# The last 64 contraction rows of a gated feed-forward as two half-array tiles

## Chip, cores and metric

The kernel runs on one core of a Trainium2 chip. The metric is device time in microseconds (us); before, three runs gave a median of 827.28 us (827.27 to 827.48).

## What is computed

The input x has 2048 rows of 448 columns, float32. Each row is normalised to xn. From xn come a Fourier mixing s and a gated feed-forward g, and the output is x + s * g.

```python
xn = layernorm(x)
a, b = xn @ hid_re.T, xn @ hid_im.T
s = seq_re @ a - seq_im @ b
g = silu((gelu(xn @ w_gate) * (xn @ w_up)) @ w_down)
out = x + s * g
```

The gate and up weights are 448 x 1792, the down weight 1792 x 448; the sequence matrices are 2048 x 2048. This case is about the two products `xn @ w_gate` and `xn @ w_up`, whose contraction has 448 rows: three tiles of 128 and a rest of 64.

## The kernel before

**Split operands.** Every float32 operand is split into two float32r parts, a high part h and a low part l. ScalarE (ACT) copies the operand into h with rounding, VectorE (DVE) subtracts to get l. A product is h\*h + h\*l + l\*h, summed in one PSUM bank. For a contraction of 448 rows that makes 3 x 3 = 9 full passes for the first 384 rows. The last 64 rows are stored twice, in partitions 0 to 63 and again in 64 to 127 of the fourth tile, on both sides. For the weights the first copy holds h and the second l (`prep_w`, L137), so that two full passes, one against xn's high part and one against its low part, do h\*h, l\*h, h\*l and l\*l of these rows. One tile of gate or up therefore takes 11 passes (`gu_mm`, L154 to L164).

**Tiling.** The 2048 rows form four chunks c of 512; xn is held transposed in SBUF for all of them, as xth[c] and xtl[c]. The hidden width 1792 is 14 tiles f of 128, worked off in seven groups of two (`GROUPS`). For each tile and chunk there are two PSUM banks, pg[0] for gate and pg[1] for up. They come from a pool of four banks (`ps_mm`). `act` (L170) then applies gelu to the gate on ACT, multiplies by up on DVE, and splits the result into h and l of hs (L172, L175, L176, L177).

**Down.** `down` (L190) multiplies hs by the down weights: four row tiles kk, six passes of 448 columns each, and DVE adds the sum of each into gacc (L210; in group 0 it copies, L208). The banks are two of `ps_o` and two of `ps_tp`; in group 0 only the two of `ps_o`. Functions in the list `between` are called behind the row tiles, which places other engines' work among down's.

**Order.** Every engine runs its instructions in the order in which they are written. After a start that is written out by hand (L215 to L342), a loop runs over the groups gi and chunks c (L346 to L385). One round before is: gate and up of the group's first tile, `down` of the previous round (`prev`), preparation of something for the next group (the weights of its two tiles in rounds 1 and 2, its down weights in round 3; in the last group the hidden-DFT matrices eh and el), then gate and up of the second tile with its `act`. SyncE (SP) issues all DMAs; the load for a preparation is issued at the head of its round into one of three raw buffers.

**The start.** L338 prepares the first weight of group 1. Its copy runs on ACT, its two subtractions on GpSimd (POOL). Behind it stand the Newton step of the layernorm (L89 to L93) and the norms of chunk 3 (L101), three on DVE and one on POOL.

**After the loop** come the hidden products (`hid_mm`, L401) with 22 passes per row tile, which read eh[0] to eh[3] in turn. The first of them is issued ahead of the last `down`. Then come the sequence products (L466 to L468).

Of the kernel before, what the change touches and what calls it, by code (L numbers as in the profile page):

```python
# [13 lines left out]
P = 128  # L14
S = 2048
D = 448
DX = 512             # D and its last 64 columns again
F = 1792
NK = S // P          # 16 row tiles; row r = p * 16 + k
NC = 4               # chunks of four row tiles  # L20
NF = F // P          # 14 tiles of the hidden width
EPS = 1e-5
WARM = 10
GROUPS = [(f, f + 1) for f in range(0, NF, 2)]
# [1 line left out]

@with_exitstack
def fnet_geglu(ctx: ExitStack, tc: tile.TileContext, x, ct, et, wgu, wd, out):
    """xn = layernorm(x); s = Cr (xn ErT) - Ci (xn EiT);
    g = silu((gelu(xn Wg) * (xn Wu)) Wd); out = x + s * g.  # L30

    float32 operands of products are split into two float32r parts, h + l, exactly; a product is
    h*h + h*l + l*h in one PSUM accumulation. A contraction of 448 rows is three tiles of 128 and
    one of 64, whose h*h and l*h (and h*l and l*l) share a tile.

    Every engine runs its instructions in the order in which they stand here."""
    nc = tc.nc

    xv = x.rearrange("p (k d) -> p k d", k=NK)
# [11 lines left out]
    def big(shape, dt, name):  # L51
        return bigp.tile(shape, dt, name=name, tag="big")
# [7 lines left out]
    def split(h, l, src):  # L60
        nc.scalar.activation(h, src, AF.Copy)  # L61
        nc.vector.tensor_sub(l, src, h)  # L62

# [1 line left out]
    xr, xth, xtl = [None] * NC, [None] * NC, [None] * NC  # L65

    def load_x(c, k0, k1):
# [4 lines left out]
    def stats(c, k0, n):  # L72
        st = const.tile([P, 4, 6], F32, name=f"st{c}_{k0}", tag="st", bufs=2)
        mv = const.tile([P, 4, 2], F32, name=f"mv{c}_{k0}", tag="mv", bufs=3)
        sd = const.tile([P, 4, 4], F32, name=f"sd{c}_{k0}", tag="sd", bufs=3)

        def one(i):
            nc.vector.bn_stats(st[:, i], xr[c][:, k0 + i, :D])  # L78
            nc.vector.bn_aggr(mv[:, i], st[:, i])

        def root():
            r, t, w = sd[:, :n, 0], sd[:, :n, 1], sd[:, :n, 2]
            nc.scalar.activation(t, mv[:, :n, 1], AF.Sqrt, bias=epst)
            nc.vector.tensor_scalar(w, mv[:, :n, 1], EPS, -0.5, op0=ALU.add, op1=ALU.mult)  # L84
            nc.vector.tensor_scalar_mul(sd[:, :n, 3], mv[:, :n, 0], -1.0)

        def newton():
            r, t, w = sd[:, :n, 0], sd[:, :n, 1], sd[:, :n, 2]
            nc.vector.reciprocal(r, t)  # L89
            # one Newton step: r * (1.5 - 0.5 * (var + eps) * r * r)  # L90
            nc.vector.tensor_mul(t, r, r)  # L91
            nc.vector.tensor_mul(t, t, w)
            nc.vector.scalar_tensor_tensor(r, t, 1.5, r, op0=ALU.add, op1=ALU.mult)  # L93

        def norm(i, eng=nc.vector):
            v = xr[c][:, k0 + i]
            if eng is nc.scalar:
                eng.activation(v, v, AF.Identity, bias=sd[:, i, 3:4])
                eng.activation(v, v, AF.Copy, scale=sd[:, i, 0:1])
            else:  # L100
                eng.tensor_scalar(  # L101
                    v, v, mv[:, i, 0:1], sd[:, i, 0:1], op0=ALU.subtract, op1=ALU.mult
                )

        return one, root, newton, norm
# [12 lines left out]
        xth[c] = big([P, 4, 512], FR, f"xth{c}")  # L118
        xtl[c] = big([P, 4, 512], FR, f"xtl{c}")

# [1 line left out]
    def load_w(f):  # L122
        raw = raw_tile(f"wraw{f}")
        nc.sync.dma_start(raw, wgu[f].rearrange("p k g f -> p (k g f)"))
# [2 lines left out]
    def prep_w(f, raw, copy=None, sub=None):  # L127
        w = big([P, 1792], FR, f"w{f}")
        wh, wl = w[:, :1024], w[:, 1024:]
        if copy is None:  # L130
            nc.scalar.activation(wh, raw, AF.Copy)
        else:
            copy(wh, raw)
        sub = sub or nc.vector.tensor_sub
        sub(wl, raw[:, :768], wh[:, :768])
        # the last 64 contraction rows: h below, l above
        sub(wh[64:, 768:], raw[64:, 768:], wh[64:, 768:])  # L137
        return wh, wl

    def load_d(grp):  # L140
# [7 lines left out]
    def prep_d(grp, rv, sub=None):  # L148
        w = big([P, 2, 2, D], FR, f"d{grp[0]}")
        nc.scalar.activation(w[:, 0], rv, AF.Copy)  # L150
        (sub or nc.vector.tensor_sub)(w[:, 1], rv, w[:, 0])
        return w

    def gu_mm(ps, w, g, c, cols, late_xtl=False):  # L154
        wh, wl = w
        hs = [wh[:, (2 * k + g) * P : (2 * k + g + 1) * P] for k in range(4)]
        ls = [wl[:, (2 * k + g) * P : (2 * k + g + 1) * P] for k in range(3)]
        hh = [(hs[k], xth[c], k) for k in range(3)]
        hl = [(hs[k], xtl[c], k) for k in range(3)]
        lh = [(ls[k], xth[c], k) for k in range(3)]  # L160
        last = [(hs[3], xth[c], 3), (hs[3], xtl[c], 3)]
        mm = hh + lh + last[:1] + hl + last[1:] if late_xtl else hh + hl + lh + last
        for n, (a, xt, k) in enumerate(mm):
            nc.tensor.matmul(ps[:, cols], a, xt[:, k, cols], start=n == 0, stop=n == len(mm) - 1)  # L164

    def gu_ps(f, c):
        pool, tag = (ps_o, "po") if (f, c) == (0, 1) else (ps_mm, "mm")
# [12 lines left out]
    def gateup(f, c, w, hs, between=()):  # L180
        pg = gu_ps(f, c)
        for g in range(2):
            gu_mm(pg[g], w, g, c, slice(0, 512))
            if g < len(between):
                between[g]()
        return act(f, c, pg, hs)
# [24 lines left out]
            if kk < len(between):  # L211
                between[kk]()

# [1 line left out]
    with tc.manual_schedule():  # L215
        load_x(0, 0, 1)
        load_x(0, 1, 2)
# [14 lines left out]
        tbl = const.tile([P, 1], F32, name="tbl")  # L232
        nc.scalar.activation(tbl, epst, AF.Sqrt)

        # keep the tensor engine's clock up while the first rows come in
        warm = ps_o.tile([P, 512], F32, name="warm", tag="po")
        for _ in range(WARM):
            nc.tensor.matmul(warm, junk[:, :P], junk, start=True, stop=True)
# [96 lines left out]
        one(3)  # L335
        l1()
        root()
        nws = [prep_w(GROUPS[1][0], w_raw[0], None, nc.gpsimd.tensor_sub)]  # L338
        newton()
        for i in range(4):  # L340
            norm(i, nc.gpsimd if i == 3 else nc.vector)
        prev = (0, 1, wdn, hs1)  # L342

# [1 line left out]
        eh, el = [], []  # L345
        for gi, grp in enumerate(GROUPS):  # L346
            nxt = GROUPS[gi + 1] if gi + 1 < len(GROUPS) else None
            if gi > 0:
                nws = []
            for c in range(NC) if gi > 0 else range(2, NC):  # L350
                if nxt and c in (1, 2):
                    raw = load_w(nxt[c - 1])
                elif nxt and c == 3:
                    raw = load_d(nxt)
                elif not nxt:
                    raw = raw_tile(f"eraw{c}")[:, : 2 * D]
                    nc.sync.dma_start(raw, et[c].rearrange("p r d -> p (r d)"))
                hs = big([P, 2, 2, 512], FR, f"hs{gi}_{c}")
                m0, h0, l0 = gateup(grp[0], c, ws[0], hs[:, 0])
                between, between1 = [lambda: (m0(), h0()), l0], []  # L360
                if (gi, c) == (0, 2):
                    new_xt(3)
                    turn = lambda k: turn_split(*turn_mm(3, k))
                    between = [between[0], lambda: (l0(), turn(0)), lambda: turn(1), lambda: turn(2)]
                    between1 = [lambda: turn(3)]
                down(*prev, between)
                if nxt and c in (1, 2):
                    nws.append(prep_w(nxt[c - 1], raw))
                elif nxt and c == 3:
                    nwdn = prep_d(nxt, raw)  # L370
                elif not nxt and c < 3:
                    eh.append(ring_tile(f"eh{c}", 0))
                    el.append(ring_tile(f"el{c}", 1))
                    split(eh[c][:, : 2 * D], el[c][:, : 2 * D], raw)
                elif not nxt:
                    eh.append(raw_tile("eh3", FR))
                    nc.scalar.activation(eh[3][:, : 2 * D], raw, AF.Copy)
                    nc.vector.tensor_sub(eh[3][64:, : 2 * D], raw[64:], eh[3][64:, : 2 * D])
                m1, h1, l1 = gateup(grp[1], c, ws[1], hs[:, 1], between1)
                m1()  # L380
                h1()
                l1()
                prev = (gi, c, wdn, hs)
            if nxt:
                ws, wdn = nws, nwdn  # L385

# [1 line left out]
        ab = [None] * NK  # L388

        def hid_mm(k):  # L390
# [20 lines left out]
                l[:, 1], ps[1], -1.0, h[:, 1], op0=ALU.mult, op1=ALU.subtract  # L411
            )

        # pieces of Cr, Ci: four row tiles of s by one of t
        pieces = [(tt, q) for tt in range(NK) for q in range(4)]
        c_raw, c_hl = {}, {}

# [30 lines left out]
        hid_split(NK - 1, ps)  # L448
        load_c(2)

# [1 line left out]
        for n, (tt, q) in enumerate(pieces):  # L452
            load_c(n + 3)
            split_c(n + 2)
# [60 lines left out]
```

## Time and profile before

| | |
|---|---|
| median of three runs | 827.28 us |
| the profiled execution, first to last instruction (span) | 825.4 us |
| TensorE passes (PE) and weight loads (PEld) | 3932 each |
| mean granted TensorE clock | 0.996 of full |
| one chunk of a later group | 14.87 us |

The profiled execution's own time is known only as this span; what the runs have beyond it, 1.9 us of the median, lies around the first and last instruction.

Times of rows are in us from the span's start. In a timeline row the first number is the start and the second the length of a run of like instructions, xN their count, and the bracket the idle time before them with what ended it. In a row of grouped instructions the last figures are busy time in us, mean ns of one, and idle time before them. L164 is line 164 of the kernel. PE is TensorE's matmul, PEld its weight load, which overlaps it. The ends of matmuls are modelled by the profiler.

### The profile page before, as it was taken

How to read it: one execution, taken by the hardware profiler on the slowest of the kernel's cores; microseconds unless marked ns; L12 is line 12 of the kernel's file. 1: busy time of each engine (PE TensorE's matmuls, PEld its weight loads, DVE VectorE, ACT ScalarE, POOL GpSimd, SP SyncE). 2: the span in 40 equal slices, each digit the busy share in tenths (PEclk: the TensorE clock that was granted, in tenths of full speed). 3: DMA queues.
4: the chain of work that ended last, by engine and by line, in shares of the span. 5: the costliest groups of instructions: out<-in, count | busy, mean ns of one | idle time of the engine just before them, and what ended most of it. 6: DMA issues, size and time to landing. Idle time of an engine off the chain costs nothing.

```text
span 825.4 us, 9169 instructions
## 1 busy us (share of the span) xinstructions
PE 815.2 (99%) x3932; PEld 727.9 (88%) x3932; DVE 311.6 (38%) x464; ACT 204.7 (25%) x280; POOL 46.3 (6%) x30
## 2 busy tenths in 40 slices
PE   7999999999999999999999999999999999999998
PEld 6988888888888888888889999999999999999997
DVE  7983433434334343353443233222323322222321
ACT  3552122121212221222221223122222222222220
POOL 3120000000000000000000000011111111111110
PEclk8999999999999999999999999999999999999999
DMA  8011010010000000001010002344444434343442
GB/s 343 8 40 34 1 52 22 5 48 23 25 26 23 26 25 23 23 23 44 1 47 6 0 26 61 92 138 146 144 136 134 135 125 125 125 125 124 125 125 60
DMA packets 19369, 58.07 MB, mean 70 GB/s; under 512 B 2048, under 2 KB 8064, under 8 KB 18944
## 3 DMA queue, kind: packets, MB, share of 16 engines
q1 hardware_dynamic: 19328, 57.48, 22.0%
q8 instruction: 31, 0.51, 0.3%
q14 instruction: 10, 0.08, 0.0%
HBM read 53.81 MB, written 3.67 MB: 70 GB/s over the span
## 4 chain that ended last, share of the span: by engine, by line
PE 96%; DVE 2%; DMA 1%; issue 0%; ACT 0%; SPq 0%
PE gu L164 33%; PE po L201 16%; PE py L467 13%; PE py L466 13%; PE py L468 13%; PE ab L401 9%; DMA xr<-x 1%; DVE xr L101 1%; PE pt L110 1%; DVE xtl L62 0%; DVE st L78 0%; DVE sd L84 0%; DVE ga L208 0%; DVE sd L91 0%; SPq L70 0%
## 5 line engine op out<-in xcount | busy, mean ns | idle before, releaser
L164 PE MATMUL gu<-xth,w 128*128 128x512 f32 (+1 forms) x826 | 218.9, 383 | 1.9 <-ACT xth L61 1.9
L466 PE MATMUL py<-ab,c 128*128 128x448 f32 x512 | 187.0, 365 | 0.0
L468 PE MATMUL py<-ab,c 128*128 128x448 f32 x512 | 187.0, 365 | 0.0
L467 PE MATMUL py<-ab,c 128*128 128x448 f32 x512 | 187.0, 365 | 0.0
L164 PEld LDWEIGHTS gu<-xth,w 128*128 128x128 f32 x826 | 152.4, 191 | 30.3 <-ACT xth L61 2.1
L201 PE MATMUL po<-d,hs 128*128 128x448 f32 x672 | 142.1, 366 | 1.3 <-DVE ga L208 1.3
L164 PE MATMUL gu<-xtl,w 128*128 128x512 f32 (+1 forms) x472 | 140.8, 381 | 0.0
L201 PEld LDWEIGHTS po<-d,hs 128*128 128x128 f32 x672 | 125.8, 188 | 12.6 <-DVE ga L208 1.5
L62 DVE TENSOR_TENSOR c<-raw,c 128x1024 fp32r<-128x1024 f32 x64 | 78.3, 1224 | 138.1 <-ACT c L61 136.2
L61 ACT ACTIVATE c<-raw 128x1024 fp32r<-128x1024 f32 x64 | 67.9, 1061 | 224.3 <-DMA raw<-ct 217.4
L468 PEld LDWEIGHTS py<-ab,c 128*128 128x128 f32 x512 | 96.2, 188 | 7.6
L466 PEld LDWEIGHTS py<-ab,c 128*128 128x128 f32 x512 | 96.2, 188 | 7.6
L467 PEld LDWEIGHTS py<-ab,c 128*128 128x128 f32 x512 | 96.2, 188 | 7.6
L164 PEld LDWEIGHTS gu<-xtl,w 128*128 128x128 f32 x472 | 87.7, 191 | 16.9
L210 DVE TENSOR_TENSOR ga<-ga,po 128x448 f32<-128x448 f32 x96 | 59.5, 620 | 110.2 <-PE po L201 110.2
L176 ACT ACTIVATE hs<-gt 128x512 fp32r<-128x512 f32 x56 | 35.4, 632 | 180.0 <-DVE gt L175 180.0
L175 DVE TENSOR_TENSOR gt<-gt,gu 128x512 f32<-128x512 f32 x56 | 38.3, 684 | 89.7 <-PE gu L164 89.7
L473 POOL TENSOR_TENSOR ga<-ga,xres 128x448 f32<-128x448 f32 x15 | 31.0, 2067 | 719.2 <-DVE ga L472 719.2
L172 ACT ACTIVATE gt<-gu 128x512 f32<-128x512 f32 x56 | 33.4, 599 | 119.6 <-PE gu L164 119.6
L177 DVE TENSOR_TENSOR hs<-gt,hs 128x512 fp32r<-128x512 f32 x56 | 38.8, 694 | 20.2 <-ACT hs L176 18.3
L472 DVE TENSOR_TENSOR ga<-ga,py 128x448 f32<-128x448 f32 (+1 forms) x17 | 10.1, 594 | 86.5 <-PE py L468 86.5
L401 PE MATMUL ab<-eh,xth 128*128 128x448 f32 x128 | 31.1, 365 | 0.0
(56 smaller groups left out, 332.3 us busy)
## 6 DMA issues: line engine op xcount, KB each, us to landing
raw<-ct SPq DMA_DIRECT2D x64, 512.0 KB, 4.9
wraw<-wgu SPq DMA_DIRECT2D x14, 512.0 KB, 3.6
xres<-x SPq DMA_DIRECT2D x16, 224.0 KB, 5.2
out<-ga SPq DMA_DIRECT2D x15, 224.0 KB, 2.0
draw<-wd SPq DMA_DIRECT2D x7, 448.0 KB, 3.5
xr<-x SPq DMA_DIRECT2D x3, 1024.0 KB, 12.3
eraw<-et SPq DMA_DIRECT2D x4, 448.0 KB, 3.4
xr<-x SPq DMA_DIRECT2D x2, 256.0 KB, 2.9
```

The costliest lines, as they stand in the source:

```text
L61: nc.scalar.activation(h, src, AF.Copy)
L62: nc.vector.tensor_sub(l, src, h)
L164: nc.tensor.matmul(ps[:, cols], a, xt[:, k, cols], start=n == 0, stop=n == len(mm) - 1)
L175: lambda: nc.vector.tensor_mul(gt, gt, pg[1]),
L176: lambda: nc.scalar.activation(hs[:, 0], gt, AF.Copy),
L177: lambda: nc.vector.tensor_sub(hs[:, 1], gt, hs[:, 0]),
L201: nc.tensor.matmul(po[:, :D], hs[:, i, part, kk * P : (kk + 1) * P], wdn[:, b, i], start=n == 0, stop=n == 5,)
L210: nc.vector.tensor_add(ga, ga, po[:, :D])
L401: nc.tensor.matmul(p[:, :D], a, b, start=n == 0, stop=n == len(mm) - 1)
L466: nc.tensor.matmul(py[:, :D], a, h, start=k + r == 0, stop=False)
L467: nc.tensor.matmul(py[:, :D], a, l, start=False, stop=False)
L468: nc.tensor.matmul(py[:, :D], b, h, start=False, stop=q == 3 and i == 7)
```

## The change

Groups 1 to 6 get another way of doing gate and up; group 0, and with it the start, keeps the old one.

- A weight is now split in full: `prep_w_halves` makes h and l for all 1024 columns (one ACT copy, one DVE subtraction), in place of h and 768 columns of l with a packed rest. It is used for all weights from group 1 on, so the first of them (L338) has its subtraction moved from POOL to DVE.
- `gu_main` issues the nine full passes of one tile of gate or up. `gu_tails` issues the last 64 rows of one hidden tile: three products, each for gate on partitions 0 to 63 and for up on partitions 64 to 127, six passes of 64 contraction rows in alternation. The term l\*l of these rows is no longer summed.
- A round is now: the full passes of both tiles, the half passes of both tiles, gelu and product of both, `down` of the previous round with the low parts of hs placed among its sums, then the preparation (`prepare`, which holds the old code).

The comments and the docstring go as well.

```diff
+    def prep_w_halves(f, raw):
+        w = big([P, 2048], FR, f"w{f}")
+        wh, wl = w[:, :1024], w[:, 1024:]
+        nc.scalar.activation(wh, raw, AF.Copy)
+        nc.vector.tensor_sub(wl, raw, wh)
         return wh, wl
...
+    def gu_main(ps, w, g, c):
+        wh, wl = w
+        sl = [slice((2 * k + g) * P, (2 * k + g + 1) * P) for k in range(3)]
+        mm = [(wh, xth[c]), (wh, xtl[c]), (wl, xth[c])]
+        for n, (a, xt) in enumerate(mm):
+            for k in range(3):
+                nc.tensor.matmul(ps, a[:, sl[k]], xt[:, k], start=n + k == 0, stop=False)
+
+    def gu_tails(pg, w, c):
+
+        wh, wl = w
+        mm = [(wh, xth[c]), (wh, xtl[c]), (wl, xth[c])]
+        for n, (a, xt) in enumerate(mm):
+            for g in range(2):
+                rows = slice(64 * g, 64 * g + 64)
+                nc.tensor.matmul(
+                    pg[g], a[rows, (6 + g) * P : (7 + g) * P], xt[rows, 3],
+                    start=False, stop=n == 2,
+                )
...
-        nws = [prep_w(GROUPS[1][0], w_raw[0], None, nc.gpsimd.tensor_sub)]
+        nws = [prep_w_halves(GROUPS[1][0], w_raw[0])]
         newton()
...
+        def prepare(nxt, c, raw):
+            if nxt and c in (1, 2):
+                nws.append(prep_w_halves(nxt[c - 1], raw))
+            elif nxt and c == 3:
+                nwdn.append(prep_d(nxt, raw))
...
                 hs = big([P, 2, 2, 512], FR, f"hs{gi}_{c}")
+                if gi > 0:
+                    pgs = [gu_ps(f, c) for f in grp]
+                    for i in range(2):
+                        for g in range(2):
+                            gu_main(pgs[i][g], ws[i], g, c)
+                    for i in range(2):
+                        gu_tails(pgs[i], ws[i], c)
+                    m0, h0, l0 = act(grp[0], c, pgs[0], hs[:, 0])
+                    m1, h1, l1 = act(grp[1], c, pgs[1], hs[:, 1])
+                    m0()
+                    m1()
+                    h0()
+                    h1()
+                    down(*prev, [l0, l1])
+                    prepare(nxt, c, raw)
+                    prev = (gi, c, wdn, hs)
+                    continue
                 m0, h0, l0 = gateup(grp[0], c, ws[0], hs[:, 0])
```

More of the change, by code (lines that the diff above doesn't have):

```diff
@@ L138, in prep_w @@
         return wh, wl
+    def prep_w_halves(f, raw):
[3 more added lines that the diff above has]
+        nc.vector.tensor_sub(wl, raw, wh)
+        return wh, wl
     def load_d(grp):
@@ L345, in fnet_geglu @@
         eh, el = [], []
+        def prepare(nxt, c, raw):
[3 more added lines that the diff above has]
+                nwdn.append(prep_d(nxt, raw))
+            elif not nxt and c < 3:
+                eh.append(ring_tile(f"eh{c}", 0))
+                el.append(ring_tile(f"el{c}", 1))
+                split(eh[c][:, : 2 * D], el[c][:, : 2 * D], raw)
+            elif not nxt:
+                eh.append(raw_tile("eh3", FR))
+                nc.scalar.activation(eh[3][:, : 2 * D], raw, AF.Copy)
+                nc.vector.tensor_sub(eh[3][64:, : 2 * D], raw[64:], eh[3][64:, : 2 * D])
         for gi, grp in enumerate(GROUPS):
@@ L349, in fnet_geglu @@
                 nws = []
+            nwdn = []
             for c in range(NC) if gi > 0 else range(2, NC):
@@ L366, in fnet_geglu @@
                 down(*prev, between)
[L367 to L378, printed above, removed]
+                prepare(nxt, c, raw)
                 m1, h1, l1 = gateup(grp[1], c, ws[1], hs[:, 1], between1)
@@ L384, in fnet_geglu @@
             if nxt:
-                ws, wdn = nws, nwdn
+                ws, wdn = nws, nwdn[0]
         ab = [None] * NK
```

## The prediction

> **What bounds the kernel now.** I read the page's part 1 first, then its part 4, then the chain in order of time.
>
> ```profile
> span 825.4 us, 9169 instructions
> PE 815.2 (99%) x3932; PEld 727.9 (88%) x3932; DVE 311.6 (38%) x464; ACT 204.7 (25%) x280; POOL 46.3 (6%) x30
> PE gu L164 33%; PE po L201 16%; PE py L467 13%; PE py L466 13%; PE py L468 13%; PE ab L401 9%; DMA xr<-x 1%; DVE xr L101 1%; PE pt L110 1%; DVE xtl L62 0%; DVE st L78 0%; DVE sd L84 0%; DVE ga L208 0%; DVE sd L91 0%; SPq L70 0%
> ```
>
> TensorE is busy 99% of the span and carries 96% of the chain that ended last. Every other engine is at 38% or less. A pass taken from TensorE shortens the kernel and a pass added lengthens it, wherever no new wait arises. A third of the chain is L164, the products that the change rewrites. Next, the chain in order of time, in the steady part:
>
> ```profile
> 81.93 4.86 PE po L201 x24
> 86.79 10.00 PE gu L164 x44
> 96.79 4.86 PE po L201 x24
> ```
>
> One chunk of a later group is 44 passes of gate and up in 10.00 us and 24 of down in 4.86 us, without a gap: **0.2273 us a pass** (10.00/44) and 0.2025 us a down pass. The busy time by stretch says the same from another side: its columns are the length, then PE, PEld, DVE, ACT and POOL busy, then the clock. The chunk takes 14.87 us, the clock is fully granted, DVE works 6.36 of it and ACT 3.41.
>
> ```profile
> 111.66:126.53 14.87, 14.87 (x69) 12.77 (x69) 6.36 (x10) 3.41 (x5) 0.00 (x0) 1.00 0.13 36
> L164 PE MATMUL gu<-xth,w 128*128 128x512 f32 x742 | 203.3, 390 | 0.0
> ```
>
> The second row gives the tail of a pass: one runs 0.390 us by the profile's model though the next starts after 0.2273, so it is still under way **0.163 us** (0.390 - 0.2273) after its successor could enter.
>
> **What the change removes.** In groups 1 to 6 there are 6 x 4 = 24 chunks. Each tile of the hidden width had 2 x 11 = 22 full passes per chunk, 4 of them for the last 64 rows. It gets 18 full passes and 6 half-array ones, which make 3 pairs if the two halves run at once. For the two tiles of a chunk that is 44 passes before against 36 plus 6 pairs. If a pair costs one pass, 2 passes go per chunk: 24 x 2 x 0.2273 = **-10.91 us**.
>
> **Does a pair cost one pass?** It needs two weight loads. The start of the kernel, where passes are short, shows how close loads can come.
>
> ```profile
> 16.70 0.46 PEld L110 LDWEIGHTS pt<-ident,xr 128*128 128x128 f32 x4
> 19.39 0.91 PEld L164 LDWEIGHTS gu<-xth,w 128*128 128x128 f32 x7
> L110 PEld LDWEIGHTS pt<-ident,xr 128*128 128x128 f32 x64 | 7.4, 140 | 3.0 <-issue 1.5 <-PE pt L110 0.5
> L164 PEld LDWEIGHTS gu<-xth,w 128*128 128x128 f32 x826 | 152.4, 191 | 30.3 <-ACT xth L61 2.1 <-POOL w L135 0.2
> ```
>
> Four loads of 0.140 us in 0.46 us start 0.107 apart, seven of 0.191 in 0.91 start 0.120 apart. A pair's two loads thus take 0.214 to 0.240 us, about the 0.2273 of a pass. I take 0.2273 and keep for the range that the loads bind: 24 x 6 x 0.013 = +1.8 us. The loads also set the halves apart: the second half's weights come one load after the first's, so the last half pass of a chunk ends about 0.11 us late. 24 x 0.11 = **+2.6 us**; 0 if both loads slip in ahead. The Trainium skill (TensorE: Matmul & The Clock Gate, Part 3) has row tiles start about 4 ns apart. With that my sum would be some 2.5 us lower; no row here shows half passes.
>
> **The switch, on which the sign hangs.** A chunk now goes from full passes to half ones and back, 48 times in all. No row of before shows such a switch. Two are near it: transposes between products, and TensorE starting again after a wait.
>
> ```profile
> 16.80 0.60 PE L110 MATMUL pt<-ident,xr 128*128 128x128 f32 x4
> 17.73 0.63 PE L110 MATMUL pt<-ident,xr 128*128 128x128 f32 x4 [0.33 <-DVE xr L101]
> 18.11 0.60 PE L164 MATMUL gu<-xth,w 128*128 128x256 f32 x3
> 17.70 0.42 PEld L110 LDWEIGHTS pt<-ident,xr 128*128 128x128 f32 x4 [0.54 <-PE pt L110]
> L110 PE MATMUL pt<-ident,xr 128*128 128x128 f32 x64 | 9.2, 274 | 1.4 <-issue 1.0 <-DVE xr L101 0.3
> ```
>
> Of the four transposes at 17.73 the last starts at 18.09 at the latest (17.73 + 0.63 - 0.274), and the product follows at 18.11. Changing the kind of pass costs nothing there. That is the **lower end, 0**; nothing suggests a gain. But those passes use the whole array alike. A half pass wants the array's two halves to sum apart; as I see it (an argument, not a row), the full passes must first be through. The **upper end** is then the tail and a whole exposed load: 0.163 + 0.191 = 0.354 us. After the wait the load shows at 17.70 and its transpose at 17.73, and the burst is 0.03 longer than the one at 16.80: an exposed load cost about 0.06. The ends lie far apart; I take the tail with this small load, 0.163 + 0.06 = **0.223 us**, since the tail is the nearest row to a full array emptying. 48 x 0.223 = **+10.7 us**. The Trainium skill (TensorEngine Tiling, Key Properties) says that changing the tiling mode drains TensorE, which speaks against this change; it gives no price, and no run here shows it. If instead the transposes' row is the right guide, this term is nothing.
>
> **The other edits.** Two places lose cover.
>
> First, the last chunk. Gate and up of the second tile stood between the preparation of eh3 (L377, L378) and the hidden products (L401). Now down stands directly ahead of them.
>
> ```profile
> 426.90 0.94 ACT L377 ACTIVATE eh<-eraw 128x896 fp32r<-128x896 f32 x1
> 428.56 0.86 PE L164 MATMUL gu<-xth,w 128*128 128x512 f32 x3
> 428.76 0.62 DVE L210 TENSOR_TENSOR ga<-ga,po 128x448 f32<-128x448 f32 x1 [0.51 <-PE po L201]
> 429.41 1.09 DVE L378 TENSOR_TENSOR eh<-eraw,eh 64x896 fp32r<-64x896 f32 x1
> ```
>
> On before's clock, down's passes are issued by 428.56; DVE finishes down's last sum, then writes eh3 until 429.41 + 1.09 = 430.50. The hidden products would start at 428.56 and need eh3 at their fourth pass, 3 x 0.2025 later, at 429.17. Late by **1.3 us**, once; bounds 0 and 2.
>
> Second, the preparation of the first weight of group 1 (L338): its subtraction goes from POOL to DVE, ahead of the newton step and the norms, and waits there for ACT's copy.
>
> ```profile
> 34.64 1.83 DVE L101 TENSOR_SCALAR xr<-xr,mv,sd 128x512 f32<-128x512 f32 x3
> 48.03 1.05 ACT L131 ACTIVATE w<-wraw 128x1024 fp32r<-128x1024 f32 x1
> 48.16 0.18 DVE L89 RECIPROCAL sd<-sd 128x4 f32<-128x4 f32 x1 [0.77 <-ACT sd L83]
> 48.98 3.41 DVE L101 TENSOR_SCALAR xr<-xr,mv,sd 128x512 f32<-128x512 f32 x3
> 49.16 2.08 POOL L135 TENSOR_TENSOR w<-wraw,w 128x768 fp32r<-128x768 f32 x1 [12.10 <-ACT w L131]
> 52.31 0.61 DVE L208 COPY ga<-po 128x448 f32<-128x448 f32 x1
> 52.98 1.48 PE L201 MATMUL po<-d,hs 128*128 128x448 f32 x6 [1.29 <-DVE ga L208]
> L62 DVE TENSOR_TENSOR c<-raw,c 128x1024 fp32r<-128x1024 f32 x64 | 78.3, 1224 | 138.1 <-ACT c L61 136.2
> ```
>
> DVE now waits for the copy until 49.08, subtracts 1.22 (to 50.30), does newton in the 0.82 it took (48.16 to 48.98; to 51.12) and the norms. Those took 3.41 us beside POOL's subtraction and 1.83 without it, so they end at 52.95 instead of 52.39: the shorter norms pay back most. Queued behind them is the copy of down's first bank, and TensorE already waits 1.29 us for that: **+0.6 us**, up to 2.1 if the norms stay at 3.41. POOL, rid of the subtraction, starts its own norm as soon as newton is done; SP's next weight load waits for the raw buffer, which now comes free at 50.3, a gain with no one behind it.
>
> ```profile
> 91.91 0.69 DVE L175 TENSOR_TENSOR gt<-gt,gu 128x512 f32<-128x512 f32 x1 [4.46 <-PE gu L164]
> 94.40 0.60 ACT L172 ACTIVATE gt<-gu 128x512 f32<-128x512 f32 x1 [1.13 <-PE gu L164]
> ```
>
> Elsewhere I cost nothing. The gelus of both tiles wait for the end of the half passes, and the next full passes need their four PSUM banks: two gelus of 0.60 and two products of 0.69 fit into the 4.86 us of down. Without down between, they would cost about 2 us a chunk. The split of hs moves between down's sums, and a chunk of full passes lies ahead of its reader. DVE has 6.36 us of work in a chunk of some 14.9. The later weights' one subtraction of 1.22 replaces two, behind down's sums, a chunk or more ahead of use; no DMA is added or moved past another queue's work.
>
> **Sum:** -10.91 + 2.64 + 10.70 + 1.33 + 0.6 = +4.4 us on the profiled span of 825.4. The median shown is 827.28, so 1.9 us lie around the span and I leave them as they are. Forecast **831.6 us**.
>
> **Rivals.**
>
> A, my forecast: halves overlap, each switch costs about the tail. With 0.163 a switch the sum is 828.8; with 0.354 and loads that bind (+6.3 + 1.8) it is 839.7. Chance 0.46.
>
> B, on the other side: the array changes over as it does for transposes, nothing waits. Then 831.6 - 10.7 = **820.9**, and 818.3 with no skew. It decides where a switch costs under (10.91 - 2.64 - 1.93)/48 = 0.13 us. For it speaks the gapless row at 18.11; against it that no pass there uses half an array. Chance 0.34.
>
> C: the halves do not run at once. 12 half passes of 0.2273 follow each other where 8 full ones stood: 24 x 4 x 0.2273 = +21.8, with +1.9 **851.0**, or 861.7 with switches of 0.223. For it: each pass in this trace starts one pass-time after the one before. Against: they use the same rows, so nothing else was possible. Chance 0.12.
>
> D: a switch empties only part of the tail, 0.10 to 0.163 us: 825.7 to 828.8, about **827.2**. Chance 0.08.
>
> **Chances and range.** A measurement of this kernel tells about 0.2% (1.65 us) from no change. Faster is B and a little of D: 0.36. Same is most of D and A's lowest edge: 0.07. Slower is the rest of A, and C: 0.57. The range takes in A, B and D, 818 to 840, and leaves out C. Cases of both signs hold most of the chance; the likeliest one's own range is 828.8 to 840.
>
> **What would show it.** A chunk of a later group is 14.87 us now. It should be about 14.87 - 0.45 + 0.56 = 14.97 in A, 14.5 in B, 15.8 or more in C. In a chunk's timeline A shows the first half pass, and the first down pass, 0.2 us later than one pass-time behind the pass ahead; B no such gap; C half passes 0.23 apart where A and B have two within that time. The hidden products should show one wait of 1.3 us for DVE on L378's line, and the wait of down's passes for DVE near 53 us should grow from 1.29 to about 1.9. I am wrong if a switch costs less than 0.13 us, or if gelu or its product shows up as TensorE's releaser in every chunk.

## The result, and the profile after

The changed kernel takes **828.56 us** (median of seven runs, 828.38 to 830.02) against 827.27 us for the kernel before in the same runs: a ratio of 1.0021, 95% interval 1.0012 to 1.0031. It is slower, by 1.3 us where I had forecast 4.4. That is about the 0.2% which a measurement of this kernel can just tell from no change. The profiled execution's span is 826.4 us against 825.4.

The page's first lines and its chain of work:

```profile
span 826.4 us, 9391 instructions
PE 814.3 (99%) x4028; PEld 714.6 (86%) x4028; DVE 308.5 (37%) x454; ACT 204.4 (25%) x280; POOL 43.6 (5%) x28
PE gu L181 24%; PE po L230 17%; PE py L517 13%; PE py L519 13%; PE py L518 13%; PE ab L452 9%; PE gu L190 5%; PE gu L173 4%; DMA xr<-x 1%; PE pt L112 1%; DVE xr L103 1%; DVE xtl L64 0%; DVE st L80 0%; DVE sd L86 0%; DVE w L146 0%
```

TensorE is as full as before and still carries the chain. It has 96 more passes (4028 - 3932), in hardly more time. Gate and up is now three lines: L181 the full passes, L190 the half passes, L173 the old way of group 0. One chunk in the chain in order of time:

```profile
92.43 8.17 PE gu L181 x36
100.60 1.58 PE gu L190 x9
102.18 5.07 PE po L230 x24
107.25 8.17 PE gu L181 x36
```

A chunk takes 107.25 - 92.43 = **14.82 us**, against 14.87 before: almost nothing gained, where two passes of 0.2273 were taken out. (The chain names nine of the twelve half passes; the others ran beside them.) The timeline of TensorE at the same place shows why; the second fence is its weight loads:

```profile
100.21 0.39 PE L181 MATMUL gu<-xth,w 128*128 128x512 f32 x1
100.53 0.50 PE L190 MATMUL gu<-xth,w 64*128 64x512 f32 x2
100.87 0.40 PE L190 MATMUL gu<-xtl,w 64*128 64x512 f32 x2
101.10 0.63 PE L190 MATMUL gu<-xth,w 64*128 64x512 f32 x4
101.56 0.39 PE L190 MATMUL gu<-xtl,w 64*128 64x512 f32 x2
101.80 0.39 PE L190 MATMUL gu<-xth,w 64*128 64x512 f32 x2
102.12 0.67 PE L230 MATMUL po<-d,hs 128*128 128x448 f32 x2
```

```profile
100.53 0.19 PEld L190 LDWEIGHTS gu<-xth,w 64*128 64x128 f32 x2 [0.35 <-issue]
100.64 0.19 PEld L190 LDWEIGHTS gu<-xtl,w 64*128 64x128 f32 x2
100.87 0.42 PEld L190 LDWEIGHTS gu<-xth,w 64*128 64x128 f32 x4
101.33 0.19 PEld L190 LDWEIGHTS gu<-xtl,w 64*128 64x128 f32 x2
101.57 0.19 PEld L190 LDWEIGHTS gu<-xth,w 64*128 64x128 f32 x2
102.12 0.50 PEld L230 LDWEIGHTS po<-d,hs 128*128 128x128 f32 x3 [0.36 <-issue]
```

Read the starts. Two half passes are done in the 0.39 to 0.40 us of one, and pairs follow each other (101.80 - 100.87)/4 = 0.2325 apart: the halves do run at once. Going in, the first pair starts 0.32 us behind the last full pass (0.09 more than 0.2273), and its row is 0.10 longer than the other pairs'; the second pair starts 0.34 behind the first (0.11 more than 0.2325). Together that is 0.20 us. The weight loads go with it: PEld stood idle for 0.35 us with nothing to wait for ("issue"), and the first loads of the half passes start at 100.53 together with their passes, not ahead of them under the last full pass. Whether the late load causes the gap, or both wait for the same thing, the rows don't say. Coming out it is the same: 102.12 - 101.80 = 0.32, and two down passes in 0.67 us, about 0.10 more than such a pair takes elsewhere (0.365 + 0.2025).

A preparation is covered when TensorE has other passes to do meanwhile. The two places that lose cover, the start first (DVE, then TensorE), then the last chunk:

```profile
49.27 1.22 DVE L146 TENSOR_TENSOR w<-wraw,w 128x1024 fp32r<-128x1024 f32 x1 [1.72 <-ACT w L145]
...
51.23 1.83 DVE L103 TENSOR_SCALAR xr<-xr,mv,sd 128x512 f32<-128x512 f32 x3
...
53.65 1.48 PE L230 MATMUL po<-d,hs 128*128 128x448 f32 x6 [1.14 <-DVE ga L237]
...
434.05 1.09 DVE L388 TENSOR_TENSOR eh<-eraw,eh 64x896 fp32r<-64x896 f32 x1
...
435.19 0.47 PE L452 MATMUL ab<-eh,xth 128*128 128x448 f32 x1 [1.22 <-DVE eh L388]
```

Down's passes in the start go on at 53.65 instead of 52.98. The down ahead of them began at 48.82 instead of 48.65, so 0.17 us of this lies before the change's first instruction, and 0.5 us is its own. The hidden products stand idle for 1.22 us until eh3 is there.

### The profile page after: what moved, and what is told of

The parts are those of the page before. It is cut to its first block, busy times and chain, and to the rows that moved or that the text cites. A ratio compares the mean times of both kernels' runs of the same rounds, so it can differ in the third digit from the quotient of the medians.

```text
span 826.4 us, 9391 instructions
## 1 busy us (share of the span) xinstructions
PE 814.3 (99%) x4028; PEld 714.6 (86%) x4028; DVE 308.5 (37%) x454; ACT 204.4 (25%) x280; POOL 43.6 (5%) x28
## 4 chain that ended last, share of the span: by engine, by line
PE 96%; DVE 2%; DMA 1%; issue 0%; ACT 0%; SPq 0%
PE gu L181 24%; PE po L230 17%; PE py L517 13%; PE py L519 13%; PE py L518 13%; PE ab L452 9%; PE gu L190 5%; PE gu L173 4%; DMA xr<-x 1%; PE pt L112 1%; DVE xr L103 1%; DVE xtl L64 0%; DVE st L80 0%; DVE sd L86 0%; DVE w L146 0%
## 5 line engine op out<-in xcount | busy, mean ns | idle before, releaser
L181 PE MATMUL gu<-xth,w 128*128 128x512 f32 x576 | 150.3, 389 | 0.0
L230 PE MATMUL po<-d,hs 128*128 128x448 f32 x672 | 144.6, 370 | 1.1 <-DVE ga L237 1.1
L230 PEld LDWEIGHTS po<-d,hs 128*128 128x128 f32 x672 | 123.9, 188 | 19.2 <-issue 4.7
L181 PEld LDWEIGHTS gu<-xth,w 128*128 128x128 f32 x576 | 108.1, 188 | 21.4
L181 PE MATMUL gu<-xtl,w 128*128 128x512 f32 x288 | 80.9, 389 | 0.0
L181 PEld LDWEIGHTS gu<-xtl,w 128*128 128x128 f32 x288 | 54.1, 188 | 11.5
L173 PE MATMUL gu<-xth,w 128*128 128x256 f32 (+1 forms) x154 | 34.8, 350 | 2.3 <-ACT xth L63 2.3
```

The lines of the kernel that those rows point to most:

```text
L181: nc.tensor.matmul(ps, a[:, sl[k]], xt[:, k], start=n + k == 0, stop=False)
L230: nc.tensor.matmul(po[:, :D], hs[:, i, part, kk * P : (kk + 1) * P], wdn[:, b, i], start=n == 0, stop=n == 5,)
```

## The experiments

The theory after the result: every change between full and half passes costs TensorE about 0.195 us, 48 times; pairs are as good as a pass; the order of the round itself costs nothing; and two covers are lost, once each. Each kernel ran beside the kernel before, whose median lay between 827.3 and 827.7 us in the different rounds, so that differences of a few tenths between kernels of different rounds mean little. Two of the kernels have only two timed runs (one half only; six gate, six up), four switches has four (837.9 to 845.6), the others five to eleven.

| kernel | median us | ratio to before, 95% interval | a chunk, us |
|---|---|---|---|
| full passes, new order | 830.1 | 1.0034 [1.0023, 1.0044] | 14.87 |
| the same, covers mended | 827.65 | 1.0000 [0.9991, 1.0009] | 14.87 |
| four switches a chunk | 839.3 | 1.0159 [1.0126, 1.0192] | 15.24 |
| one half only | 861.4 | 1.0414 [1.0369, 1.0459] | 16.20 |
| three gate, three up | 828.7 | 1.0021 [1.0009, 1.0033] | 14.82 |
| six gate, six up | 846.9 | 1.0234 [1.0182, 1.0285] | 15.39 |
| covers mended | 826.7 | 0.9990 [0.9981, 0.9998] | 14.82 |
| only eh3 earlier | 826.95 | 0.9990 [0.9981, 0.9998] | 14.82 |
| only the start mended | 828.0 | 1.0003 [0.9994, 1.0011] | 14.82 |
| a block for three tiles | 824.0 | 0.9959 [0.9946, 0.9971] | 14.72 on average |

**Full passes in the new order.**

```diff
-        for n, (a, xt) in enumerate(mm):
+        for n, xt in enumerate((xth[c], xtl[c])):
             for g in range(2):
-                rows = slice(64 * g, 64 * g + 64)
                 nc.tensor.matmul(
-                    pg[g], a[rows, (6 + g) * P : (7 + g) * P], xt[rows, 3],
-                    start=False, stop=n == 2,
+                    pg[g], wh[:, (6 + g) * P : (7 + g) * P], xt[:, 3],
+                    start=False, stop=n == 1,
                 )
...
-        nws = [prep_w_halves(GROUPS[1][0], w_raw[0])]
+        nws = [prep_w(GROUPS[1][0], w_raw[0])]
...
-                nws.append(prep_w_halves(nxt[c - 1], raw))
+                nws.append(prep_w(nxt[c - 1], raw))
```

> The changed kernel's order, with the last 64 rows again in full 128-row passes (the packed weights of before). Theory (each switch between full and half passes costs about 0.195 us, the order itself nothing, and two covers are lost once): a chunk of a later group takes 14.87 us as before, no gap ahead of or behind the last passes, and only the lost covers remain, 1.2 us at eh3 and 0.5 us in the start: 827.3 + 1.7 = 829.0 us. Rival (the gaps come from the new order, gelu or PSUM banks late): the gaps stay and a chunk takes about 14.87 + 0.39 = 15.26 us, in all about 838 us.

The chain in order of time, with the last full passes as L187:

```profile
102.14 1.81 PE gu L187 x8
103.95 4.86 PE po L227 x24
108.81 8.19 PE gu L181 x36
117.00 1.81 PE gu L187 x8
```

A chunk is 117.00 - 102.14 = 14.86 us, the gaps are gone (8 passes in 1.81, and no step behind them): the gaps go with the half passes and not with the order. The time, though, came out 1.1 us above what I expected. The granted clock by stretch (the columns are length, PE, PEld, DVE, ACT and POOL busy, clock, DMA share, GB/s) shows where it went in the profiled execution (830.9 us):

```profile
50.00:53.50 3.50, 1.66 (x10) 1.03 (x8) 3.33 (x10) 0.76 (x2) 2.29 (x1) 1.00 0.38 149
53.50:57.00 3.50, 3.44 (x12) 3.06 (x13) 2.96 (x6) 1.36 (x3) 0.05 (x1) 0.56 0.00 1
```

TensorE was busy for 1.66 of 3.5 us around the stop in the start, and then got 0.56 of its clock for the next 3.5. In the changed kernel's own profile the clock held at this place (1.00). The other nine runs (828.7 to 832.2 us) left no profile, so how much of the median's 1.1 us this explains is not shown.

**The same with both covers mended.** The edit is against the kernel just shown.

```diff
-        nws = [prep_w(GROUPS[1][0], w_raw[0])]
+        nws = [prep_w(GROUPS[1][0], w_raw[0], None, nc.gpsimd.tensor_sub)]
...
                         gu_tails(pgs[i], ws[i], c)
+                    if not nxt and c == 3:
+                        prepare(nxt, c, raw)
...
-                    prepare(nxt, c, raw)
+                    if nxt or c < 3:
+                        prepare(nxt, c, raw)
```

> The new order with full passes for the last 64 rows, and both covers mended (eh3 prepared ahead of the last gelus, the first weight's subtractions on POOL). Theory: the order itself costs nothing, so this is before again: 827.3 us, a chunk 14.87 us, no wait for eh3. Rival (the order costs something of its own, as the 830.1 us of the kernel with full passes may say, 1.1 us over what I expected): 828.4 us or more.

A ratio of 1.0000, interval 0.9991 to 1.0009: the new order costs nothing of its own that these runs can tell (0.7 us at most by the interval), and what the kernel above had too much goes with the lost covers.

**Four switches a chunk.**

```diff
                     for i in range(2):
                         for g in range(2):
                             gu_main(pgs[i][g], ws[i], g, c)
-                    for i in range(2):
                         gu_tails(pgs[i], ws[i], c)
```

> The changed kernel with each tile's half passes right behind its own full passes: four switches a chunk in place of two, the same passes. Theory (0.195 us a switch): 24 x 2 x 0.195 = +9.4 us, 838.0 us, a chunk 15.22 us. Rival (a fixed price per chunk, from down or from the semaphores behind the half passes): 828.6 us. With the price that I had forecast, 0.223 us and 0.11 us for halves set apart, 24 x (0.446 + 0.11) = +13.3 us, 841.9 us.

```profile
92.17 4.09 PE gu L181 x18
96.26 0.90 PE gu L190 x6
97.16 4.30 PE gu L181 x18
101.46 0.89 PE gu L190 x5
102.35 5.06 PE po L230 x24
107.41 4.09 PE gu L181 x18
```

The chunk is 107.41 - 92.17 = 15.24 us, 0.42 more than in the changed kernel for two more switches: **0.21 us each**. The price stands in single rows too: 18 full passes take 4.09 us behind down, but 4.30 behind half passes. The median is 839.3 (four runs, 837.9 to 845.6) where the theory said 838.0 and a fixed price per chunk 828.6. The theory rests on this experiment: twice the switches, about twice the price.

**All half passes on the same half.**

```diff
-                rows = slice(64 * g, 64 * g + 64)
+                rows = slice(0, 64)
```

> The changed kernel with the half passes of up on partitions 0 to 63 as well, so that all twelve of a chunk use the same half of the array. Theory (passes run side by side only on different halves): twelve in a row at 0.232 us in place of six pairs, 24 x 6 x 0.232 = +33.4 us, 862 us; the two gaps of a chunk stay. Rival (64-row passes pair whichever half they use): 828.6 us.

```profile
94.02 8.17 PE gu L181 x36
102.19 2.96 PE gu L190 x12
105.16 5.06 PE po L230 x24
110.22 8.17 PE gu L181 x36
```

861.4 us; twelve half passes stand on the chain, and the chunk is 110.22 - 94.02 = 16.20 us, 1.38 more for six steps: 0.23 us for each pass that finds no partner. So it is the two halves of the array that make a pair, and my rival C is what happens without them.

**Gate first, up behind it.** In the changed kernel gate and up alternate. First, three of each:

```diff
-        for n, (a, xt) in enumerate(mm):
-            for g in range(2):
+        for g in range(2):
+            for n, (a, xt) in enumerate(mm):
                 rows = slice(64 * g, 64 * g + 64)
```

> The changed kernel with a tile's three gate half passes issued first and its three up half passes behind them, in place of alternation. Theory (passes start in the order of issue, and two run together only as neighbours on different halves): nine steps of 0.232 us in place of six per chunk, 24 x 3 x 0.232 = +16.7 us, 845 us. Rival (a half that is free takes its next pass past the queue): 828.6 us. Without any running together it would be 862 us.

The theory fell here: 828.7 us, and a chunk of 14.82. The program issues the passes of gate against xth, xtl, xth and then those of up; the profile shows them started in twos all the same:

```profile
99.96 0.50 PE L190 MATMUL gu<-xth,w 64*128 64x512 f32 x2
100.29 0.40 PE L190 MATMUL gu<-xtl,w 64*128 64x512 f32 x2
100.53 0.63 PE L190 MATMUL gu<-xth,w 64*128 64x512 f32 x4
```

A pass for a half that is free passes the ones that wait for the other half. So what is said at the top, that every engine runs its instructions in the order in which they are written, does not hold for half passes on different halves. Then all six of gate before all six of up (`gu_tails` called for g = 0 on both tiles, then for g = 1):

> The changed kernel with the six gate half passes of both tiles of a chunk issued first and the six up half passes behind them. Three of each in this way changed nothing, so a free half does take its pass past the queue. Theory (the two halves work off their passes independently, and far enough ahead for six): 828.6 us, six pairs. Rival (only a few passes ahead, three): the up passes begin when three gate passes have gone, nine steps in place of six, 24 x 3 x 0.23 = +16.6 us, 845 us. Only neighbours: eleven steps, +27.6 us, 856 us.

```profile
102.90 0.49 PE L190 MATMUL gu<-xth,w 64*128 64x512 f32 x1
103.24 0.39 PE L190 MATMUL gu<-xtl,w 64*128 64x512 f32 x1
103.47 0.63 PE L190 MATMUL gu<-xth,w 64*128 64x512 f32 x3
103.81 0.51 PE L190 MATMUL gu<-xtl,w 64*128 64x512 f32 x2
```

Two start alone, and a second one comes in beside the third: the rival that allows a few passes ahead is nearest. A chunk is 15.39 us, 0.57 more, which is two and a half steps and not three. When up's first pass got in, three gate passes were waiting ahead of it; that it can pass three and not four is my reading of this one kernel. The two timed runs were 842.4 and 851.5 us, and 24 x 0.57 = 13.7 us accounts for the lower; what the profiled one (851.5) has beyond it is told in the last section.

**Covers mended**, with the half passes: the first weight's subtraction back on POOL, and eh3 prepared ahead of the last gelus (the edits of the second kernel, with `sub` handed to `prep_w_halves`).

> The changed kernel with both covers mended: eh3 is prepared ahead of the gelus of the last round, and the first weight's subtraction is back on POOL. Theory: the waits of 1.2 us (hidden products for eh3) and 0.5 us (start) go, chunks stay at 14.83 us: 828.6 - 1.7 = 826.9 us, within 0.2% of before. Rival (the waits are only the face of something later that binds as well): 828.6 us as it was.

826.7 us, 1.9 below the changed kernel where 1.7 was expected; no wait for eh3 is left. And each by itself, the last chunk and the start:

> The changed kernel with only eh3 prepared earlier; the first weight's subtraction stays on DVE. Theory: the wait of 1.2 us goes and nothing else, 828.6 - 1.2 = 827.4 us. Rival (that wait stands in for the end of down, or the clock): 828.6 us.

> The changed kernel with only the first weight's subtraction back on POOL; eh3 stays late. Theory: 0.5 us of waiting in the start goes, 828.6 - 0.5 = 828.1 us, and the wait for eh3 stays at 1.2 us. Rival (in some executions the longer stop in the start also lets the clock fall, as the profile of the kernel with full passes shows, 1.7 us): up to 2 us less in such executions, so that the median falls by more than 0.5 and the spread shrinks.

826.95 and 828.0 us: 1.6 and 0.6 below the changed kernel, for 1.2 and 0.5 expected. These two ran in another round, in which the kernel before was 0.4 us slower; set against the kernel before they are about 2 and 1 us below, and the intervals are 0.7 us or more to either side, so the medians can't settle gains of this size. The traces are closer. With eh3 prepared early, the last two calls of down start 437.60 - 428.08 = 9.52 us apart in the chain, against 439.30 - 428.29 = 11.01 in the changed kernel: 1.5 us gained. With the start mended, down's passes in the start go on 53.20 - 48.74 = 4.46 us after the first of them, against 53.65 - 48.82 = 4.83: 0.4 us gained. The rival of the second, a clock that falls in some executions, does not show in the median, which is nowhere near 2 us lower, nor in a smaller spread (1.7 us against 1.6). That it takes part in single runs is not excluded.

**One block for three tiles.** The block of half passes finishes one tile and begins the next two, whose full passes come after it; gate and up get six PSUM banks and down two. 16 blocks do the work of 24.

```diff
...
+            if n % 3 == 0:
+                pgu[n] = banks(n)
+            for g in range(2):
+                gu_main(pgu[n][g], wts[gi][i], g, c, n % 3 == 0, n % 3 != 0)
+            if n % 3 == 0:
+                for j in (n, n + 1, n + 2):
+                    gj, cj, ij = units[j]
+                    if j > n:
+                        pgu[j] = banks(j)
+                    gu_tails(pgu[j], wts[gj][ij], cj, j > n, j == n)
+            m, h, l = act(grp[i], c, pgu.pop(n), hs[:, i])
...
```

> Covers mended, and one block of half passes for every three tiles in place of two: the block finishes one tile and begins the next two, whose full passes follow; two banks more for gate and up, two less for down. 16 blocks in place of 24. Theory: 16 switches fewer, 16 x 0.195 = 3.1 us below the kernel with the covers mended: 826.9 - 3.1 = 823.8 us, 0.4% below before. Rival (the price goes with the half passes, not with the switches): 826.9 us. Another: down with two banks waits for DVE, and the gain goes into that wait: 826 us or more with waits on down's line.

```profile
92.16 8.19 PE u L181 x36
100.34 2.29 PE u L190 x18
102.63 5.06 PE po L230 x24
107.69 8.19 PE u L181 x36
115.88 4.87 PE po L230 x24
120.74 4.11 PE u L181 x18
124.85 2.29 PE u L190 x18
127.14 4.31 PE u L181 x18
131.45 4.86 PE po L230 x24
```

**824.0 us, 0.41% faster than before** (interval 0.29 to 0.54%), and 2.7 us below the kernel with covers mended, against 3.1 expected. Three chunks take 131.45 + 4.86 - 92.16 = 44.15 us, 14.72 each. The second chunk in these rows has no block, and its down follows the full passes without a step: 8.19 and 4.87. In the third, 18 full passes take 4.11 us ahead of the block and 4.31 behind it: a switch is 0.20 us here as well. No down pass of the later groups waits for DVE; two banks are enough.

## Why the prediction was right and wrong

**Right in size, not in its parts: the switch.** A switch costs, and in about the size of the gain, so that the sum hangs on small terms. 0.223 us was forecast; the timeline gives 0.20 for going in, the experiment with four switches 0.21, and 0.195 each closes the chunk: 36 x 0.2273 + 6 x 0.2325 + 4.86 + 2 x 0.195 = 14.83. 48 x 0.195 is 9.4 us in place of 10.7. My split of it, 0.163 for the tail and 0.06 for an exposed load, was not what the trace shows: the first half passes start some 0.09 late, and run some 0.10 longer. I had taken the whole modelled tail, and a load's price from a burst of transposes; the two errors nearly cancelled, which was luck. My argument that the full passes must first be through isn't borne out by the modelled ends either: the last full pass starts at 100.21 and runs 0.39, to 100.60, and the first half passes start at 100.53. What makes TensorE wait at a switch stays open; its price is shown. Rival B falls with the gaps, C with the pairs, and D with the price, 0.195 and not 0.163 or less. The time itself, 828.56, lies just below the 828.8 at which A's own range began and inside D's, because the next term was nothing.

**Wrong: the halves set apart.** This is the step that failed. The term of +2.6 us, that the second half's weights come one load after the first's, measured 0. I had read the spacing of loads from full-array rows, 0.107 to 0.120 us, and carried it to loads for different halves. These start together: two of them are done in 0.19 us at 100.53, the time of one, and the two passes of a later pair, at 101.80, stand in one row of 0.39 us, again the time of one. No last half pass comes 0.11 us late. The 4 ns of the Trainium skill (TensorE: Matmul & The Clock Gate, Part 3), which I named and didn't use, is what agrees with these rows. This step is most of the difference between +4.4 and the result.

**Nearly right: a pair costs a pass.** 0.2325 against 0.2273: 24 x 6 x 0.0052 = +0.75 us, inside the 1.8 that I had kept for the range.

**Right: the two covers.** eh3 was forecast at 1.33. The idle time is 1.22 in the trace, and with only this mended the chain there is 1.5 us shorter. The start was forecast at 0.6; the trace of the changed kernel gives 0.5, that of the kernel with only this mended 0.4. The stop named for the start did not grow as forecast: the wait for the first bank was 1.14 us and not about 1.9, since the transposes ahead of it came later as well.

With the measured terms the sum is -10.91 + 0.75 + 9.4 + 1.22 + 0.5 = **+1.0 us** on the profile. The profile shows +1.0 (825.4 to 826.4), of which 0.17 lies ahead of the change's first instruction, so the sum closes to a few tenths of a us. The gain of the change is real, 10 us of passes, and it is paid back at the 48 places where the array changes over. The direction was right; the time is in the range; the size was three times too large, for the halves set apart and for 1.3 us too much in the switches.

## What to carry to other kernels

Every block of half-array passes pays for two switches, however many passes it saves, so longer blocks keep more of the saving. Here a block saved two passes, which just paid for its two switches. Count the switches first, and then look for an order with fewer of them, for instance by beginning the next tiles' sums in the same block. Work that is moved together uncovers what lay between: for each preparation, look for what stood ahead of its reader, and move it into the idle time of its engine.

## What the hardware showed that was not expected

The halves of the array take their passes out of the order of issue: three gate passes ahead of three up passes cost nothing (828.7 us), six ahead of six cost 0.57 us a chunk (15.39 against 14.82).

The same full passes can run at a slightly different pace for a long part of an execution. In the profiled execution of the kernel with six gate passes first, every product from the restart behind the wait for eh3 (450.67 us) to the end was slower, at full clock and without a wait: 330 hidden products in the chain take 68.20 us where the changed kernel takes 66.88, and of the sequence products 341 passes stand in a stretch of 70 us where the changed kernel has 347. These are the rows of the changed kernel and then of that one:

```profile
530.00:600.00 70.00, 70.00 (x347) 64.87 (x346) 19.20 (x18) 15.26 (x17) 8.27 (x4) 1.00 0.45 140
```

```profile
530.00:600.00 70.00, 70.00 (x341) 63.58 (x340) 20.20 (x21) 18.95 (x21) 6.18 (x3) 1.00 0.43 136
```

This is about 2% over 330 and 1536 passes, 1.3 and some 6 us. Ahead of the wait there is no such difference: 24 down passes take 5.06 us and 36 full passes 8.17 in both kernels. The profiled span of that kernel is 849.6 us, so this pace belongs to its time of 851.5, and it is most of the 9.1 us between its two runs. Most of what is left is the clock in the start, told next. That the other run had neither is only inferred from the sum; it left no profile. What sets the pace was not tried and stays open.

A stop of TensorE in the start can cost more than its length. With 1.66 us busy in the 3.5 us from 50.0 on, the granted clock was 0.56 in the next 3.5 us (the first experiment). In the profile of the kernel with six gate passes first the busy time was 2.26 us, and the clock then 0.67 and, from 57 to 60, 0.81; its first half passes start at 87.57 where those of the kernel with one half only, with the same 2.26 us busy and a clock of 1.00, start at 86.00, 1.6 us earlier. In these two profiles the bursts of TensorE's passes from 45.64 to 53.87 start within 0.01 us of each other. The changed kernel kept 1.00 with 2.04 us busy, the one with three gate passes first with 1.89. So neither the busy time in this stretch nor the order of the passes ahead of it decides it. Two of the twelve profiles show such a fall; what sets it off, and how often it happens in other runs, was not measured.
